# Order edges in the first phase of a three-stage kernel: exponentials behind an eviction, and VectorE side work behind x's low part

## The chip, the cores and the metric

The kernel runs on one core of one Trainium2 chip. The metric is the device time of that core in microseconds (us). A profiled execution has two numbers: its time as a run, and its span, from the first to the last instruction in the trace.

## The reference

Three stages, each feeding the next; batch 4, 576 tokens, width 512.

```python
# 1. attention, 8 heads of 64, a causal window of 128 tokens
scores = 0.125 * q @ k.T + bias          # bias: -slope(head) * |distance|
scores = where(0 <= rel < 128, scores, -1e9)
x = softmax(scores) @ v                  # then [4, 576, 512]
# 2. a gated block
u, v = split(relu(x @ w_in), 2)          # w_in: 512 x 1024
v = (v - mean(v)) / sqrt(var(v) + 1e-6)
v = w_spatial @ v + b_spatial            # mixes the 576 tokens
x = (u * v) @ w_out
# 3. four experts of causal attention (head size 64); each token keeps the two
#    experts of the largest gate logits, weighted by their softmax
```

## The kernel before, in words

**Number form.** Every large product runs on TensorE with fp32 operands split in two: a high part in the rounded type fp32r and a low part, the rest. `split` (L131 to L133) does this for a tile in PSUM: ScalarE (ACT) casts the high part (L132), then VectorE (DVE) subtracts it from the source (`lo_part`, L129).

**The first phase** is the loop of lines 600 to 634. It computes stage 1 and, woven into it, the products of stage 2 up to the spatial mix. A tile is (batch b, tile j): 128 tokens, five tiles to a batch (the last has 64), 20 tiles in all. Step s of the loop does, in program order:

- `attend(tile s-2)`: 32 matmuls of attention weights by v into the PSUM tile px (L415);
- `scores(tile s)`: q by k into two PSUM tiles ps, one for each half g of the heads (L353, L356);
- `take(tile s-2)`: `split` of px into x, the input of stage 2;
- `parts(s)`: one piece of side work; and then, for g = 0 and 1, `transposes(tile s-1, g)` (four TensorE transposes into the PSUM tile pt, L390, evicted by ACT to pT, L391, and cut in two by GpSimd, L398 and L399), `softmax(tile s, g)` (DVE row reductions, L150; ACT exponentials, L151, four to a half; DVE normalisation, L378 to L380), and `parts(s)` again.

`parts` draws on three lists. `late`: chunks 4 to 7 of w_in, of which `bits` (L281 to L289) makes a rounded high part by integer operations on DVE, `add_in` puts it through TensorE with the identity (psw, L218, L219) and a cast (L221), and `low_in` makes the low part (L129). `prep` (steps 6 to 8): the spatial weights wsp, five tiles that come by DMA (L252) into st_wsp, a buffer of two, and are cast on ACT (L254) and subtracted on DVE (L129). `outw` (from step 9): the output weights.

Between these, `dense.pull` draws stage 2: `v_tile` (products pv, L436; relu on ACT, L444; statistics on DVE, L447 and L448; the square root on ACT, L462 and L463, and four small DVE operations, L466 to L469; `scale`, L472; `high`, an ACT cast, L475; `low`, L129), `u_half` (pu, L499; relu L503) and `spatial`.

**Buffers.** pt and px share one PSUM buffer (pool psT, one buffer): the transposes of tile s-1 wait until both halves of `split` have read px, each later use of pt waits for the eviction before it, and px waits for the last of these. The products pv, pu, pg and psw share three (pool psD).

**Order.** TensorE's order is written out by hand. The order on ACT, DVE, GpSimd and the DMA queue is set by a scheduler at build time from its own estimates of durations; an order edge (`tc.issue_after`) makes an instruction stand behind another in the issue order of its engine, without a semaphore.

Of the kernel before, what the change touches and what calls it, by code (L numbers as in the profile page):

```python
# [2 lines left out]

# [6 lines left out]
F32 = mybir.dt.float32  # L10
# [7 lines left out]
ALU = mybir.AluOpType  # L18
# [4 lines left out]
P = 128  # L23
# [79 lines left out]
def block_kernel(ctx, tc, qP, kP, v, w_in, wspT, bsp, w_outT, wcat, wo, rel, relt, low, tri, out):  # L103
    nc = tc.nc
# [21 lines left out]


    def lo_part(lo, src, hi, engine=nc.vector):
        engine.tensor_sub(lo, src, hi.bitcast(F32))  # L129

    def split(hi, lo, src):  # L131
        nc.scalar.copy(hi, src)  # L132
        lo_part(lo, src, hi)  # L133

    def staggered(gens):

# [39 lines left out]
    x = [xg.tile([P, 4, 640], F32R, name=f"x{i}") for i in range(2)]  # L176
    u = [d2.tile([P, S], F32, name=f"u{m}") for m in range(4)]
    vn = [[d2.tile([P, 512], F32R, name=f"vn{i}_{t}") for t in range(5)] for i in range(2)]
# [204 lines left out]
    def transposes(b, j, g):  # L383
        p = st_[b, j, g]
        n = 4 if j < 4 else 2
        pt = psT.tile([P, 4, P], F32, tag="T", name=f"pt{b}_{j}_{g}")
        here = a1.tile([P, 4, P], F32, tag="pT", name=f"pT{b}_{j}_{g}", bufs=4)
        before = None
        for i in range(n):
            nc.tensor.transpose(pt[:, i, :], p[:, i, :], ident)  # L390
        nc.scalar.copy(here[:, :n], pt[:, :n])  # L391
        if j > 0:

            before = a1.tile([P, 4, P], F32, tag="pU", name=f"pU{b}_{j}_{g}", bufs=4)
            w = P if j < 4 else 64
            m = 4
            u_, h = (t[:, :n].rearrange("p i (o q) -> p (i o) q", q=w) for t in (before, here))
            nc.gpsimd.affine_select(out=u_, in_=h, pattern=[[0, m], [-1, w]], compare_op=ALU.is_gt, fill=0.0, base=0, channel_multiplier=1)  # L398
            nc.gpsimd.affine_select(out=h[:w], in_=h[:w], pattern=[[0, m], [1, w]], compare_op=ALU.is_ge, fill=0.0, base=0, channel_multiplier=-1)  # L399
        st_[b, j, g] = (before, here)  # L400
# [18 lines left out]
    def take(b, j, px):  # L419
        q0, qn = TOK[j]  # L420
        if j < 4:
            split(x[0][:, :, q0 : q0 + P], x[1][:, :, q0 : q0 + P], px)
        else:
            twice = [t[:, :, 512:640].rearrange("p m (r c) -> p m r c", r=2) for t in x]
            split(*twice, px[:, :, :64].unsqueeze(2).to_broadcast([P, 4, 2, 64]))
        xready[b, j] = now[0] + (b == 0)

    stats_, vr = {}, {}

    def v_tile(b, t):  # L430
        t0 = TOK[t][0]
        pv = psD.tile([P, 512], F32, tag="D", name=f"pv{b}_{t}")
        n = 0
        for i, j in PASSES:
            for k in range(4):
                nc.tensor.matmul(pv, x[i][:, k, t0 : t0 + P], win[j][:, k, 512:1024], start=(n == 0), stop=(n == 11))  # L436
                n += 1
            if n < 12:
                yield 4 * 216
        if t == 0:  # L440
            stats_[0] = d2.tile([P, 5, 10], F32, tag="vs", name=f"vs{b}", bufs=2)
        st = stats_[0]
        vr[t] = d2.tile([P, 512], F32, tag="vr", name=f"vr{b}_{t}", bufs=3)
        nc.scalar.activation(vr[t], pv, AF.Relu)  # L444

        def stats():
            nc.vector.bn_stats(st[:, t, 0:6], vr[t])  # L447
            nc.vector.bn_aggr(st[:, t, 6:8], st[:, t, 0:6])  # L448

        dense.post.append(stats)  # L450
        if t in (2, 4):
            tiles = range(0, 3) if t == 2 else range(3, 5)
            dense.post.extend(normalised(st, tiles))
        yield 4 * 216

    def normalised(st, tiles):
# [12 lines left out]
            nc.vector.tensor_mul(y, y, z)  # L469

        def scale(t):
            nc.vector.tensor_scalar(vr[t], vr[t], st[:, t, 6:7], st[:, t, 8:9], op0=ALU.subtract, op1=ALU.mult)  # L472

        def high(t):
            nc.scalar.copy(vn[0][t], vr[t])  # L475
# [1 line left out]
        def low(t):  # L477

            r = slice(64, 128) if t == 4 else slice(0, 128)
            lo_part(vn[1][t][r], vr[t][r], vn[0][t][r])  # L480
            if t == 4:
                nc.scalar.copy(vn[1][t][0:64], vr[t][0:64])
                nc.gpsimd.tensor_scalar(vn[0][t][64:97], pad[64:97].to_broadcast([33, 512]), 1.0, 0.0, op0=ALU.mult, op1=ALU.add)
# [43 lines left out]
    tiles = [(b, j) for b in range(B) for j in range(5)]  # L527
    prep = setup()
# [29 lines left out]
    late = late_chunks()  # L558

    def parts(s):  # L560

        next(late, None)
        for _ in range(2 if 6 <= s < 9 else 0):
            next(prep, None)
        if s >= 9:
            next(outw, None)


    warm(22)
# [17 lines left out]
    px = attend(0, 0)  # L587
# [16 lines left out]
    outw = iter(())  # L604
    for s in range(2, len(tiles) + 2):
# [3 lines left out]
        if s == 9:  # L609
            early_stack.close()  # L610
            outw = out_weights(right.enter_context(tc.tile_pool(name="later", bufs=1, side="right")))
        if s > 2:
# [3 lines left out]
            px = attend(b, j)  # L616
# [9 lines left out]
        for g in range(2):  # L626
            if 1 <= s <= len(tiles):
                transposes(*tiles[s - 1], g)
            dense.pull(RATE / 6)
            if s < len(tiles):  # L630
                softmax(*tiles[s], g)
            now[0] += 1
            dense.pull(RATE / 6)
            parts(s)
# [321 lines left out]
    px = None  # L956
# [104 lines left out]
```

## Time and profile before

| | |
|---|---|
| time, median of 3 runs | 515.16 us (515.05 to 515.49) |
| time of the profiled execution | 514.89 us |
| its span | 513.2 us |
| mean granted TensorE clock | 0.988 |
| TensorE matmul busy | 488.0 us (95%) |
| VectorE busy | 308.4 us (60%) |
| ScalarE busy | 261.8 us (51%) |
| GpSimd busy | 98.4 us (19%) |

The profiled execution took 514.89 us as a run, 1.69 us more than its span. Busy times overlap. The granted clock is the share of TensorE's full clock that the chip allowed, averaged over the span.

### The profile page before, as it was taken

The page shows a single profiled execution, that of the slowest core. Times are in us where ns is not written, and L with a number is a line of the kernel's source. Part 1 is how long each engine was busy: PE and PEld are TensorE (multiplying, and loading weights), DVE is VectorE, ACT ScalarE, POOL GpSimd, SP SyncE. Part 2 cuts the span into 40 slices and gives each one's busy share as a digit, 9 for nine tenths or more (in the row PEclk, how much of TensorE's full clock was granted, in tenths as well). Part 3 has the DMA queues.
Part 4 walks back from the last instruction along what each step waited for, and adds up shares of the span by engine and source line. Part 5 has one row for each costly group of instructions (what it writes and reads, how often), then busy time and mean ns, then how long its engine had stood idle before and what let it go on. Part 6 is the DMA issues. An engine that isn't in the chain of part 4 may idle for free. (4 is left out here: it accounts for less than half of the span.)

```text
span 513.2 us, 10541 instructions
## 1 busy us (share of the span) xinstructions
PE 488.0 (95%) x3910; PEld 425.5 (83%) x3910; DVE 308.4 (60%) x1069; ACT 261.8 (51%) x778; POOL 98.4 (19%) x205
## 2 busy tenths in 40 slices
PE   8879889999999999999999999989989999999995
PEld 6547668898988989899888999978978898897784
DVE  4978877555878768785455525264574564562441
ACT  4764567533656337463344314264564554546652
POOL 0012210222102211012211010122322333232121
PEclk9997989999999999999999999999999999999999
DMA  8931223325231451301206640230000000003321
GB/s 283 372 128 42 63 87 102 114 70 181 91 94 43 180 189 42 94 2 52 104 1 193 198 158 5 90 93 1 1 1 3 2 1 1 1 2 116 112 103 42
DMA packets 25079, 44.34 MB, mean 86 GB/s; under 512 B 5826, under 2 KB 8258, under 8 KB 24644
## 3 DMA queue, kind: packets, MB, share of 16 engines
q1 hardware_dynamic: 24868, 43.54, 25.4%
q8 instruction: 31, 0.51, 0.4%
q10 hardware_dynamic: 160, 0.13, 0.1%
q14 instruction: 20, 0.16, 0.1%
HBM read 32.13 MB, written 11.53 MB: 85 GB/s over the span
## 5 line engine op out<-in xcount | busy, mean ns | idle before, releaser
L151 ACT ACTIVATE p<-p,st 128x128 f32<-128x128 f32 x144 | 56.3, 392 | 38.0 <-DVE st L150 38.0
L436 PE MATMUL pv<-win,x 128*128 128x512 f32 x240 | 63.9, 409 | 0.7 <-ACT x L132 0.7
L780 PE MATMUL pq<-x,W 128*128 128x288 f32 x384 | 59.4, 303 | 0.9 <-DVE k L129 0.8
L516 PE MATMUL pg<-wsp,vn 128*128 128x288 f32 x384 | 58.9, 298 | 0.1
L780 PEld LDWEIGHTS pq<-x,W 128*128 128x128 f32 x384 | 52.1, 188 | 4.8 <-issue 2.3
L499 PE MATMUL pu<-x,win 128*128 128x288 f32 x384 | 55.1, 298 | 0.0
L398 POOL TENSOR_SCALAR_AFFINE_SELECT pU<-pT 128x512 f32<-128x512 f32 (+1 forms) x32 | 22.6, 706 | 168.1 <-ACT pT L391 164.1
L158 POOL TENSOR_SCALAR pB<-pB,stB 128x128 f32<-128x128 f32 (+4 forms) x72 | 39.0, 560 | 80.1 <-DVE stB L868 65.5
L516 PEld LDWEIGHTS pg<-wsp,vn 128*128 128x128 f32 x384 | 52.9, 188 | 1.3 <-issue 1.0
L499 PEld LDWEIGHTS pu<-x,win 128*128 128x128 f32 x384 | 52.0, 188 | 1.8 <-issue 0.5
L436 PEld LDWEIGHTS pv<-win,x 128*128 128x128 f32 x240 | 43.9, 192 | 9.8 <-issue 1.0
L151 ACT ACTIVATE pB<-pB,stB 128x128 f32<-128x128 f32 (+3 forms) x64 | 35.6, 558 | 13.6 <-DVE stB L150 13.6
L150 DVE CUSTOM_DVE_ANT_0 pB<-psB,trit 128x128 f32<-128x128 f32 (+3 forms) x64 | 28.3, 485 | 11.1 <-PE psB L845 10.5
L888 PE MATMUL ptB<-ident,pB 128*128 128x128 f32 (+1 forms) x200 | 31.1, 274 | 3.9 <-POOL pB L158 3.6
L804 PE MATMUL pvB<-W,x 128*128 128x260 f32 (+1 forms) x240 | 34.7, 289 | 0.0
L804 PEld LDWEIGHTS pvB<-W,x 128*128 128x128 f32 (+1 forms) x240 | 30.1, 178 | 1.1 <-issue 1.1
L927 PE MATMUL pout<-wo,o 128*128 128x512 f32 x108 | 30.1, 410 | 1.0 <-ACT o L132 1.0
L353 PE MATMUL ps<-k,q 64*128 64x256 f32 (+1 forms) x256 | 29.8, 374 | 0.8 <-DMA k<-in_kP 0.8
L390 PE MATMUL pt<-ident,p 128*128 128x128 f32 x144 | 22.9, 277 | 7.8 <-DVE x L129 6.1
L888 PEld LDWEIGHTS ptB<-ident,pB 128*128 128x128 f32 (+1 forms) x200 | 23.7, 139 | 7.6 <-POOL pB L158 4.7
L150 DVE CUSTOM_DVE_ANT_0 p<-ps,relm 128x128 f32<-128x128 f32 x128 | 29.5, 286 | 0.7 <-DMA relm<-in_rel 0.2
L415 PE MATMUL px<-pT,v 128*64 128x128 f32 (+1 forms) x320 | 29.6, 276 | 0.0
(147 smaller groups left out, 882.0 us busy)
## 6 DMA issues: line engine op xcount, KB each, us to landing
q<-in_qP SPq DMA_DIRECT2D x20, 256.0 KB, 3.0
g_dram<-g SPq DMA_DIRECT2D x16, 288.0 KB, 2.1
raw<-in_w_in SPq DMA_DIRECT2D x8, 512.0 KB, 6.8
v<-in_v SPq DMA_DIRECT2D x16, 256.0 KB, 3.2
gf<-g_dram SPq DMA_DIRECT2D x4, 1024.0 KB, 5.3
out<-ot SPq DMA_DIRECT2D x16, 256.0 KB, 2.0
k<-in_kP SPq DMA_DIRECT2D x3, 1152.0 KB, 5.3
rawo<-in_w_outT SPq DMA_DIRECT2D x4, 512.0 KB, 4.3
```

Source lines behind the costliest of these rows:

```text
L150: nc.vector.tensor_tensor_reduce(s_view, ps_view, tab, -0.125, FLT_MAX, ALU.add, ALU.min, nm)
L151: nc.scalar.activation(s_view, s_view, AF.Exp, bias=nm, scale=-1.0, accum_out=sm)
L158: nc.gpsimd.tensor_scalar(p, p, r, 0.0, op0=ALU.mult, op1=ALU.add)
L353: nc.tensor.matmul(ps[:, o, 256 * h : 256 * h + kn], Q_[b, j][r, hp, :], K_[b][r, hp, k0 : k0 + kn], start=True, stop=True)
L415: nc.tensor.matmul(px[64 * o : 64 * o + 64, hp, :qn], V_[b, t][:kb, h * 64 : h * 64 + 64], rhs, start=(t == max(0, j - 1)), stop=(t == j))
L436: nc.tensor.matmul(pv, x[i][:, k, t0 : t0 + P], win[j][:, k, 512:1024], start=(n == 0), stop=(n == 11))
L499: nc.tensor.matmul(pu[:, :HALF], win[i][:, k, m * P : (m + 1) * P], x[j][:, k, c], start=(n == 0), stop=(n == 11))
L516: nc.tensor.matmul(pg[:, :HALF], vn[i][k][:, m * P : (m + 1) * P], wsp[j][:, k, c], start=(n == 0), stop=False)
L780: nc.tensor.matmul(pq[:, :HALF], W[i][:, k, c0 : c0 + P], G[j][:, k, c], start=(n == 0), stop=(n == 11))
L804: nc.tensor.matmul(pv[:tn, :260], G[i][:, k, COL[t] : COL[t] + tn], W[j][:, k, 512:772], start=(n == 0), stop=(n == 11))
L888: nc.tensor.transpose(pt[:kb, n, :], p[pr][:, o, c0 : c0 + kb], ident)
L927: nc.tensor.matmul(po[:tn], o2[i][:, pr, :tn], wos[j][:, pr, :], start=(n == 0), stop=(n == 5))
```

## The change

It adds order edges in the first phase and no operation. `transposes` keeps the instruction of its eviction (L391) in `turned[g]`, and the loop traces `softmax` of the next tile's half g under an order edge on it, so that its ACT instructions (the exponentials) stand behind the eviction in ACT's order. `take` keeps the low part of x (on DVE) in `taken`, and statistics, scale and low part of v, and everything in `parts`, are traced under an order edge on that: their DVE instructions stand behind x's low part, which was traced before them.

```diff
     def lo_part(lo, src, hi, engine=nc.vector):
-        engine.tensor_sub(lo, src, hi.bitcast(F32))
+        return engine.tensor_sub(lo, src, hi.bitcast(F32))
     def split(hi, lo, src):
         nc.scalar.copy(hi, src)
-        lo_part(lo, src, hi)
+        return lo_part(lo, src, hi)
+    taken, turned = [None], {}
+    def behind(ins):
+        return tc.issue_after(ins.ins) if ins is not None else nullcontext()
...
-        nc.scalar.copy(here[:, :n], pt[:, :n])
+        turned[g] = nc.scalar.copy(here[:, :n], pt[:, :n])
...
-            split(x[0][:, :, q0 : q0 + P], x[1][:, :, q0 : q0 + P], px)
+            taken[0] = split(x[0][:, :, q0 : q0 + P], x[1][:, :, q0 : q0 + P], px)
...
-            split(*twice, px[:, :, :64].unsqueeze(2).to_broadcast([P, 4, 2, 64]))
+            taken[0] = split(*twice, px[:, :, :64].unsqueeze(2).to_broadcast([P, 4, 2, 64]))
...
         def stats():
-            nc.vector.bn_stats(st[:, t, 0:6], vr[t])
-            nc.vector.bn_aggr(st[:, t, 6:8], st[:, t, 0:6])
+            with behind(taken[0]):
+                nc.vector.bn_stats(st[:, t, 0:6], vr[t])
+                nc.vector.bn_aggr(st[:, t, 6:8], st[:, t, 0:6])
...
         def scale(t):
-            nc.vector.tensor_scalar(vr[t], vr[t], st[:, t, 6:7], st[:, t, 8:9], op0=ALU.subtract, op1=ALU.mult)
+            with behind(taken[0]):
+                nc.vector.tensor_scalar(vr[t], vr[t], st[:, t, 6:7], st[:, t, 8:9], op0=ALU.subtract, op1=ALU.mult)
...
-            lo_part(vn[1][t][r], vr[t][r], vn[0][t][r])
+            with behind(taken[0]):
+                lo_part(vn[1][t][r], vr[t][r], vn[0][t][r])
...
     def parts(s):
-        next(late, None)
-        for _ in range(2 if 6 <= s < 9 else 0):
-            next(prep, None)
-        if s >= 9:
-            next(outw, None)
+        with behind(taken[0]):
+            next(late, None)
+            for _ in range(2 if 6 <= s < 9 else 0):
+                next(prep, None)
+            if s >= 9:
+                next(outw, None)
...
             if s < len(tiles):
-                softmax(*tiles[s], g)
+                with behind(turned.get(g)):
+                    softmax(*tiles[s], g)
```

The scheduler then orders all engines but TensorE anew. TensorE's and GpSimd's orders come out unchanged; 130 rows of ACT's order and 240 of DVE's differ. Lines of the changed kernel stand six or more further down (L391 becomes L397, L151 L157, L444 L450, L254 L260, L284 to L289 become L290 to L295). Numbers in the names are batch, tile and half: p0_2_1 is batch 0, tile 2, half 1.

**Place A**, ACT, step 4 of the loop, where tile (0,1) is transposed (pt0_1_0, pt0_1_1) and the exponentials of tile (0,2) are taken. Before:

```order
L391 COPY pT0_1_0_409<-pt0_1_0_408 128x512
L444 ACTIVATE vr0_0_423<-pv0_0_392 128x512
L151 ACTIVATE p0_2_1_455,st0_2_1_456<-p0_2_1_455,st0_2_1_456 128x128 x3
L221 CAST win0_100<-psw4_441 128x512
L151 ACTIVATE p0_2_1_455,st0_2_1_456<-p0_2_1_455,st0_2_1_456 128x128
L391 COPY pT0_1_1_446<-pt0_1_1_445 128x512
L281 ACTIVATE f6_551<-raw6_361 128x512
```

With the change:

```order
L397 COPY pT0_1_0_409<-pt0_1_0_408 128x512
L157 ACTIVATE p0_2_0_427,st0_2_0_428<-p0_2_0_427,st0_2_0_428 128x128 x4
L450 ACTIVATE vr0_0_423<-pv0_0_392 128x512
L227 CAST win0_100<-psw4_441 128x512
L397 COPY pT0_1_1_446<-pt0_1_1_445 128x512
L157 ACTIVATE p0_2_1_455,st0_2_1_456<-p0_2_1_455,st0_2_1_456 128x128 x4
L287 ACTIVATE f6_551<-raw6_361 128x512
```

Both evictions have moved ahead of the exponentials of their half; the cast of w_in's chunk 4 (L221) still stands between relu and the second eviction.

**Place B**, DVE, step 6 of the loop, which takes x of tile (0,2) (px0_2) and whose `parts` round chunk 7 of w_in (f7, u3, raw7, win1). Before:

```order
L284 TENSOR_SCALAR f7_625<-f7_625 128x512
L285 TENSOR_SCALAR u3_109<-f7_625 128x512
L286 SCALAR_TENSOR_TENSOR u3_109<-raw7_368,u3_109 128x512
L288 TENSOR_SCALAR f7_625<-u3_109 128x512
L129 TENSOR_TENSOR x1_105<-px0_2_595,x0_104 128x4x128
L365 COPY_PREDICATED ps0_4_0_612<-lowt_99,ps0_4_0_612 128x2x64
L289 SCALAR_TENSOR_TENSOR win1_101<-raw7_368,f7_625 128x512
```

With the change, where between the last two rows but five stand the eight rows of the reductions L156 of p0_4_0 and p0_4_1 (left out):

```order
L129 TENSOR_TENSOR x1_105<-px0_2_595,x0_104 128x4x128
L129 TENSOR_TENSOR win1_101<-psw6_590,win0_100 128x512
L290 TENSOR_SCALAR f7_625<-f7_625 128x512
L371 COPY_PREDICATED ps0_4_0_612<-lowt_99,ps0_4_0_612 128x2x64
L371 COPY_PREDICATED ps0_4_1_615<-lowt_99,ps0_4_1_615 128x2x64
L291 TENSOR_SCALAR u3_109<-f7_625 128x512
...
L292 SCALAR_TENSOR_TENSOR u3_109<-raw7_368,u3_109 128x512
L384 TENSOR_SCALAR st0_4_0_643<-st0_4_0_643 128x2
L294 TENSOR_SCALAR f7_625<-u3_109 128x512
L385 RECIPROCAL st0_4_0_643<-st0_4_0_643 128x2
L295 SCALAR_TENSOR_TENSOR win1_101<-raw7_368,f7_625 128x512
```

The low part of x is now first; the whole rounding of chunk 7, and the low part of chunk 6 (win1<-psw6), have moved behind it, the last of the rounding behind the reductions too.

**Place C**, ACT, step 8, where x of tile (0,4) is taken (px0_4), `prep` casts the spatial weights (wsp0<-st_wsp) and tile (1,0) is transposed (pt1_0_0, pt1_0_1). Before:

```order
L444 ACTIVATE vr0_3_782<-pv0_3_759 128x512
L132 CAST x0_104<-px0_4_803 128x4x128
L254 CAST wsp0_102<-st_wsp0_836 128x576
L254 CAST wsp0_102<-st_wsp1_839 128x576
L151 ACTIVATE p1_1_0_848,st1_1_0_849<-p1_1_0_848,st1_1_0_849 128x128 x3
L391 COPY pT1_0_0_842<-pt1_0_0_841 128x512
L151 ACTIVATE p1_1_0_848,st1_1_0_849<-p1_1_0_848,st1_1_0_849 128x128
L254 CAST wsp0_102<-st_wsp2_873 128x576
L151 ACTIVATE p1_1_1_901,st1_1_1_902<-p1_1_1_901,st1_1_1_902 128x128 x3
L391 COPY pT1_0_1_880<-pt1_0_1_879 128x512
```

With the change:

```order
L450 ACTIVATE vr0_3_782<-pv0_3_759 128x512
L260 CAST wsp0_102<-st_wsp0_836 128x576
L132 CAST x0_104<-px0_4_803 128x4x128
L260 CAST wsp0_102<-st_wsp1_839 128x576
L260 CAST wsp0_102<-st_wsp2_873 128x576
L260 CAST wsp0_102<-st_wsp3_877 128x576
L397 COPY pT1_0_0_842<-pt1_0_0_841 128x512
L157 ACTIVATE p1_1_0_848,st1_1_0_849<-p1_1_0_848,st1_1_0_849 128x128 x4
L260 CAST wsp0_102<-st_wsp4_937 128x576
L397 COPY pT1_0_1_880<-pt1_0_1_879 128x512
L157 ACTIVATE p1_1_1_901,st1_1_1_902<-p1_1_1_901,st1_1_1_902 128x128 x4
L450 ACTIVATE vr0_4_890<-pv0_4_862 128x512
```

The eviction of pt1_0_0 now stands ahead of its exponentials, and behind two more casts of the spatial weights, those of st_wsp2 and st_wsp3. The relu of tile (0,4) (vr0_4) stands behind the fifth cast and the second half's exponentials.

## Rows read from the trace of the kernel before

**Rows 1.** Page: busy us of each engine, share of the span, instructions.

```profile
PE 488.0 (95%) x3910; PEld 425.5 (83%) x3910; DVE 308.4 (60%) x1069; ACT 261.8 (51%) x778; POOL 98.4 (19%) x205
```

**Rows 2.** Waits of TensorE, 28 to 100 us: us in total, times, longest.

```profile
PE pt L390 <- DVE x L129: 5.0, 3, 3.7
PE px L415 <- ACT pT L391: 2.6, 1, 2.6
PE psw L219 <- DVE win L289: 0.8, 1, 0.8
```

**Rows 3.** The same view, 100 to 300 us.

```profile
PE pt L390 <- DVE x L129: 1.2, 2, 0.9
...
PE pt L390 <- ACT pT L391: 0.6, 1, 0.6
```

**Rows 4.** Windows: length, busy us PE, PEld, DVE, ACT, POOL, PEclk, DMA share, GB/s.

```profile
22.50:25.00 2.50, 1.72 (x5) 0.81 (x6) 1.85 (x6) 2.43 (x10) 0.00 (x0) 1.00 1.02 398
37.50:40.00 2.50, 2.10 (x20) 2.13 (x22) 2.43 (x7) 0.83 (x2) 1.27 (x2) 0.50 0.00 0
40.00:42.50 2.50, 2.50 (x20) 2.03 (x18) 2.36 (x6) 0.58 (x1) 0.00 (x0) 0.50 0.11 34
42.50:45.00 2.50, 2.50 (x15) 1.78 (x12) 1.84 (x7) 0.24 (x1) 0.00 (x0) 0.71 0.22 78
67.50:70.00 2.50, 2.50 (x9) 1.92 (x9) 1.76 (x11) 2.50 (x14) 0.82 (x2) 0.57 0.00 0
70.00:72.50 2.50, 2.50 (x21) 1.63 (x19) 1.40 (x4) 1.14 (x4) 1.15 (x2) 0.75 0.00 0
```

**Rows 5.** Timeline, 34 to 38 us: start, us, instruction, idle before and releaser.

```profile
34.75 0.60 PE L390 MATMUL pt<-ident,p 128*128 128x128 f32 x4
...
36.33 0.56 ACT L221 CAST win<-psw 128x512 fp32r<-128x512 f32 x1
...
37.19 0.56 ACT L391 COPY pT<-pt 128x512 f32<-128x512 f32 x1
...
37.90 0.70 PE L415 MATMUL px<-pU,v 128*64 128x128 f32 x4 [2.55 <-ACT pT L391]
```

**Rows 6.** Timeline, 52 to 58 us.

```profile
53.99 0.68 DVE L129 TENSOR_TENSOR x<-px,x 128x512 fp32r<-128x512 f32 x1
...
54.78 0.68 DVE L289 SCALAR_TENSOR_TENSOR win<-raw,f 128x512 fp32r<-128x512 uint32 x1
...
57.53 0.80 PE L219 MATMUL psw<-win,one 128*128 128x512 f32 x1
```

**Rows 7.** Windows, the stretch of place B.

```profile
51.40:57.70 6.30, 5.86 (x47) 4.63 (x43) 5.78 (x20) 3.30 (x11) 1.73 (x3) 1.00 0.28 83
```

**Rows 8.** Timeline, 62 to 67 us.

```profile
63.25 1.66 ACT L475 CAST vn<-vr 128x512 fp32r<-128x512 f32 x3 [1.42 <-DVE vr L472]
...
64.82 0.58 ACT L132 CAST x<-px 128x512 fp32r<-128x512 f32 x1
...
66.59 0.44 PE L390 MATMUL pt<-ident,p 128*128 128x128 f32 x2 [3.72 <-DVE x L129]
```

**Rows 9.** Timeline, 74 to 83 us, the stretch of place C.

```profile
74.38 0.69 DVE L129 TENSOR_TENSOR x<-px,x 128x512 fp32r<-128x512 f32 x1 [1.14 <-ACT x L132]
...
76.36 5.31 SPq L252 DMA_DIRECT2D st_wsp<-in_wspT  x4
...
78.37 0.66 PE L390 MATMUL pt<-ident,p 128*128 128x128 f32 x4 [0.30 <-ACT pT L391]
...
82.22 0.59 ACT L444 ACTIVATE vr<-pv 128x512 f32<-128x512 f32 x1
```

**Rows 10.** Tile st_wsp: the casts that read it (ns, starts), and its DMAs.

```profile
L254 ACT CAST wsp<-st_wsp x5: 659/673/674, 74.2 to 84.0; 128x576 fp32r<-128x576 f32 x5
...
DMA to landing us min/median/max: 2.6/2.8/3.7
```

**Rows 11.** Page, groups: the first phase's exponentials (busy us, mean ns; idle before, releaser).

```profile
L151 ACT ACTIVATE p<-p,st 128x128 f32<-128x128 f32 x144 | 56.3, 392 | 38.0 <-DVE st L150 38.0
```

More of the change, by code (lines that the diff above doesn't have):

```diff
@@ L1 @@
 from collections import deque
-from contextlib import ExitStack
+from contextlib import ExitStack, nullcontext
 import concourse.bass as bass
```

## Prediction

> **What bounds the kernel now.** I read the busy times first, then TensorE's waits, then the timeline and the windows around each wait. TensorE is busy for 95% of the span, the next engine for 60% [rows 1]: the kernel is bound by TensorE, and only what lets TensorE stand still or run slowly can be won. No operation is added or removed, so matmul time at full clock stays. What the change can touch lies in the first phase, up to about 300 us. There the list of waits is short. From 28 to 100 us TensorE waits 5.0 us, in three pieces, for the low part of x (the transposes use the PSUM buffer that x is read from), of which one piece is 3.7; 2.6 us once for an eviction of transposes on ACT; and 0.8 once for a rounded chunk of w_in [rows 2]. From 100 to 300 us it waits 1.2 us in two pieces for x's low part and 0.6 once for an eviction [rows 3]. The waits of the two kinds that the change speaks to, x's low part and evictions, come to 9.4 us: that is what there is to take.
>
> The second thing to see is the granted clock. After the pause of 2.6 us the clock stands at 0.50 in two windows of 2.5 us and at 0.71 in the third; after the one of 3.7 us at 0.57 and 0.75 [rows 4]. TensorE is busy there all the while, on the same matmuls, so half a clock costs half the window: 1.25 + 1.25 + 0.73, less 0.2 for the 0.4 us in which it was idle anyway, is 3.0 us for the first fall; 1.08 + 0.63 = 1.7 us for the second. Each long pause thus costs about its own length again.
>
> **The change, place A** (the 2.6 us pause). ACT cast psw at 36.33 and evicted the second transposes at 37.19, though TensorE had written them by 35.35 (34.75 + 0.60), and px, which needs the same buffer, began at 37.90, 0.71 after the eviction's start [rows 5]. Between stood exponentials of 0.39 us [rows 11], now all behind the eviction. What is left ahead of it is the cast of psw, whose matmuls stand right ahead of the transposes of 34.75 on TensorE: I let it start at 35.0, 0.56 long, so the eviction starts at 35.6 and px at 35.6 + 0.71 = 36.3. **-1.55 us**, between -2.55 (the cast no hindrance) and 0.
>
> *The clock after A.* With 0.80 + 0.95 us idle instead of 0.80 + 2.55 I take the clock to stay up: the window at 22.5 us, with 1.72 of 2.50 busy, that is 0.78 idle, kept it at 1.00 [rows 4]. **-3.0 us**, the other end 0.
>
> **Place B** (chunk 7 of w_in). DVE used to round the chunk while it waited for x's cast: four pieces before x's low part at 53.99, and the last, 0.68 at 54.78, right behind; TensorE took the chunk at 57.53, 3.5 us after x's low part began [rows 6]. Now x's low part comes first and all of the rounding stands behind it, with the low part of chunk 6 and the reductions of tile (0,4) between. DVE has 5.78 us of work in the 6.30 us of this stretch [rows 7], of which about 2 us filled the wait for x; that hole now stays empty, so the chunk comes 5.1 us after x's low part instead of 3.5. **+1.4 us** for TensorE (its 0.2 of slack taken off); bounds 0 (TensorE has that much other work that I missed) and 2.3 (the whole hole, and a piece more).
>
> **The 3.7 us pause.** ACT cast three parts of normalised v in 1.66 us, from 63.25, ahead of x's cast at 64.82; transposes began at 66.59 [rows 8]. Now one of the three casts is ahead: 2 x 0.55 = 1.1 less. Against it, two exponentials (0.39 each [rows 11]) now stand ahead of the relu from which the statistics of v come: +0.8. On DVE x's low part no longer stands behind the low parts of v: it started at 66.59 - 0.68 = 65.9 while the cast was done at 65.4, so -0.5. **-0.8 us**, between -1.6 and +0.5. A pause of 2.9 us is left, and with it, I take it, the fall of the clock (1.7).
>
> **Place C** (spatial weights). The casts of st_wsp2 and st_wsp3 now stand ahead of the eviction of pt1_0_0, and their data are not there yet: the buffer has two slots, so the third DMA can go only when DVE has made the low part of the first tile. That DMA was issued at 76.36, 2.0 after x's low part at 74.38 [rows 9]; the new order puts the low part of st_wsp0 right behind x's (which took 0.69, as I take this one to), so it is issued at 74.38 + 2 x 0.69 = 75.8, and the next at 76.5. Landing takes 2.6 to 3.7 us, 2.8 in the middle [rows 10]: st_wsp3 is there at 79.3, its cast (0.67) done at 80.0, the eviction at 80.5, and pt1_0_1, which began at 78.37 after a wait of 0.30, follows then. **+2.2 us**; the lower end 0.3, if the data come by the time the eviction is due; the upper 3.1, with the landing of 3.7.
>
> The fifth cast and four exponentials now also stand ahead of the relu of tile (0,4), which ran at 82.22 [rows 9]; that relu frees one of three PSUM buffers that the products of u_half wait for. 0.67 + 4 x 0.39 = 2.2 us later. TensorE has products in the other two buffers meanwhile, so I take 0.7 of it: **+1.55 us**, between 0 (all covered) and 2.2.
>
> **The small ones.** Of the 1.3 us in the other two waits for x's low part before 100 us [rows 2] one stays (place B) and one goes, **-0.6**. The 1.2 and 0.6 us after 100 us [rows 3] end at instructions that now come first, **-1.8**; bounds 0 and -1.8. GpSimd's order is the same and it has 81% to spare; the order on the DMA queue changes by one swap behind the phase, at no cost.
>
> **Sum:** -1.55 - 3.0 + 1.4 - 0.8 + 2.2 + 1.55 - 0.6 - 1.8 = -2.6 us. The profiled execution took 514.89, so 512.3; the median of the three runs, 515.16, stands 0.27 above it: **512.6 us**. A measurement of this kernel can tell about 0.2%, 1.0 us, from no change.
>
> **The rivals.**
>
> *R1, place C costs nothing.* The spatial weights land before the casts are reached, or the pulled products cover the wait: both terms at their lower ends, 0.3 and 0 in place of 2.2 and 1.55, so 512.6 - 3.45 = 509.1. For it: six DMAs only, and the queue's share in the stretches read is small. Against: before, ACT waited for this very data though it asked later [rows 9, 10].
>
> *R2, the change doesn't do what it says at A.* The pause shrinks, and the clock falls all the same: 512.6 + 3.0 = 515.6, no change. For it: two pauses, 0.80 and about 0.95, stand close together there. Against: 0.78 idle of 2.50 did no harm [rows 4]. The Trainium skill ("TensorE: Matmul & The Clock Gate", "A second HAM failure mode: psum-queue depth-cycling") says that short idle spells between groups of matmuls, when they are frequent, make the clock swing between its levels without one long gap. By that rule this rival holds, and the time is 515.6; the window at 22.5 us, one such spell, does not agree with it, but holds one spell and not two.
>
> *R3, the other side: the clock falls at place C.* The new pause, 2.5 us with the old 0.30, is as long as the one at A that lowered the clock. If it lowers it too, the same 3.0 us of half clock come back, and with the landing at 3.7 in place of 2.8 another 0.9: 512.6 + 3.0 + 0.9 = 516.5, slower. It decides from the point where C costs 3.6 us more than in my sum (1.0 above 515.16). For it: both pauses above 2.5 us in this trace were followed by a fall [rows 2, 4]. Against: at A 0.8 us of idle time stood right before, which C lacks, and four transposes and eight products run just ahead of it at full clock.
>
> **How the numbers follow.** Forecast 0.45, with a range of its own from 511.2 (the 3.7 us pause, now 2.9, no longer drops the clock, -1.7, some of it given back) to 514.0 (B and the relu at their upper ends); R1 0.15; R2 0.2; R3 0.2. The range, 509.5 to 517.0, leaves out about half of R1 and the upper part of R3, 0.17 together. Faster: nearly all of the forecast and R1, 0.58. Same: most of R2 and pieces of the others, 0.20. Slower: most of R3 and the rest of R2, 0.22.
>
> **What the profile after would show.** Right: no wait of px for an eviction above 1.2 us near 36 us; PEclk 1.00 in the ten us after it; the px groups there shorter than the 0.70 us of before [rows 5]; a wait of psw for win of over 1 us near 55; a wait of TensorE for an eviction of about 2.5 us near 75, and ACT idle before a cast of st_wsp for a DMA; no waits above 0.3 us for x between 100 and 300 us. Wrong: PEclk below 1 near 37 (R2), or below 1 in the 5 us after the pause at C (R3); no wait at C (R1). A new long wait at a line that I have not named would overturn the sum.

## The result: slower, and where the time went

| | before | changed |
|---|---|---|
| first comparison, median | 515.25 us (515.05 to 515.49, 4 runs) | 523.41 us (519.63 to 524.13, 4 runs) |
| ratio, 95% interval | | 1.0143 [1.0095, 1.0192] |
| repeated beside e9 and e10, median | 515.71 us (515.00 to 518.35, 17 runs) | 519.72 us (518.39 to 521.58, 7 runs) |
| ratio, 95% interval | | 1.0060 [1.0036, 1.0083] |
| profiled execution of the first comparison | 514.89 us | 524.13 us |
| its mean granted clock | 0.988 | 0.979 |

The forecast was 512.6 us with a range to 517.0. The change is slower in both comparisons, by 8.2 and by 4.0 us. At one granted clock the two agree: the one run of the first comparison with a mean of 0.989 took 519.63 us and the one of the second with 0.989 took 519.72, where 31 of 34 runs of the kernel before with 0.989 took 514.8 to 515.8. The other three of the first comparison had 0.979 and took 523.39 to 524.13. So about 4 us go with the order, and the 3.7 us between the two medians go with the clock. In the loop's own variable s, places A, B and C are at s = 2, 4 and 6; the step numbers in the section on the change are two too high.

The page of the changed kernel:

```profile
span 522.4 us, 10547 instructions
...
PE 492.2 (94%) x3910; PEld 428.6 (82%) x3910; DVE 310.1 (59%) x1069; ACT 259.5 (50%) x778; POOL 99.3 (19%) x205
```

The matmuls are the same 3910 in the same order; TensorE is busy 4.2 us longer, which is slower clock, and the rest of the 9.2 us by which the span grew (513.2 to 522.4) is idle time. Its waits, first from 28 to 100 us (to be held against [rows 2]), then from 100 to 300 us (against [rows 3]):

```profile
PE pt L396 <- DVE x L129: 3.7, 2, 3.4
PE pt L396 <- ACT pT L397: 2.5, 1, 2.5
PE psw L225 <- DVE win L295: 1.3, 1, 1.3
PE psw L224 <- DVE u L292: 0.9, 1, 0.9
PE px L421 <- ACT pT L397: 0.8, 1, 0.8
PE px L421 <- POOL pT L405: 0.6, 1, 0.6
```

```profile
PE pg L525 <- ACT vn L483: 2.2, 1, 2.2
PE pt L396 <- ACT pT L397: 1.0, 1, 1.0
PE pg L530 <- POOL vn L492: 0.9, 1, 0.9
PE pt L396 <- DVE x L129: 0.7, 2, 0.5
```

Early, the waits changed places and did not get less (8.7 us before, which is [rows 2] and the 0.30 of [rows 9]; 9.8 now). Later two waits, 3.1 us together, appear at the spatial mix of batch 3, which had none.

Since TensorE's order is the same, one matmul can be followed from one timeline to the other. The starts of six groups in the changed kernel, and two waits between them (34.87 and 54.45):

```profile
34.87 0.51 PE L225 MATMUL psw<-win,one 128*128 128x512 f32 x1 [1.26 <-DVE win L295]
...
36.63 0.44 PE L421 MATMUL px<-pU,v 128*64 128x128 f32 x4 [0.82 <-ACT pT L397]
...
47.28 0.44 PE L421 MATMUL px<-pU,v 128*64 128x128 f32 x4
...
54.45 1.13 PE L224 MATMUL psw<-u,ident 128*128 128x512 f32 x2 [0.91 <-DVE u L292]
...
55.64 0.50 PE L225 MATMUL psw<-win,one 128*128 128x512 f32 x1
...
64.04 0.69 PE L396 MATMUL pt<-ident,p 128*128 128x128 f32 x2 [3.36 <-DVE x L129]
...
79.21 0.66 PE L396 MATMUL pt<-ident,p 128*128 128x128 f32 x4 [2.49 <-ACT pT L397]
...
300.27 1.76 PE L525 MATMUL pg<-wsp,vn 128*128 128x288 f32 x12
```

Before, the six started at 37.90 [rows 5], 50.67, 57.53 [rows 6], 66.59 [rows 8], 78.37 [rows 9] and 292.38 us:

```profile
50.67 0.44 PE L415 MATMUL px<-pU,v 128*64 128x128 f32 x4
...
292.38 1.76 PE L516 MATMUL pg<-wsp,vn 128*128 128x288 f32 x12
```

So the changed kernel is 1.3 us ahead at A, 3.4 ahead at 47 us, 1.9 at 55, 2.6 at 64, then 0.8 **behind** at 79 and 7.9 behind at 300. The remaining 1.3 us come after that, most of them where the clock is at half near 353 us. The granted clock of the changed kernel, in the stretches in which it was at half (columns as in [rows 4]):

```profile
63.30:70.10 6.80, 6.06 (x16) 4.44 (x16) 6.25 (x25) 4.39 (x19) 2.33 (x4) 0.50 0.21 77
80.40:83.80 3.40, 3.40 (x15) 3.28 (x14) 1.69 (x11) 2.25 (x9) 0.00 (x0) 0.50 0.56 177
288.60:295.40 6.80, 5.91 (x25) 5.59 (x25) 4.79 (x8) 3.65 (x7) 0.62 (x1) 0.50 0.05 13
353.40:356.80 3.40, 3.37 (x14) 2.87 (x14) 0.44 (x2) 0.65 (x2) 2.66 (x7) 0.50 0.03 5
```

After A the clock stayed up; it fell towards the end of the pause for x, after place C, between the two new waits of the spatial mix, and right after a wait of 1.93 us for GpSimd that ended at 353.24. The same wait, 1.92 us to 345.33, stood in the kernel before, and no fall followed it there.

**The end of the phase, which the prediction did not look at.** ACT's order around the last casts of v, before:

```
L503 ACTIVATE u1_107<-pu3_1_1_3197 128x288
L475 CAST vn0_3_113<-vr3_3_3134 128x512
L475 CAST vn0_4_114<-vr3_4_3171 128x512
L482 CAST vn1_4_119<-vr3_4_3171 64x512
L503 ACTIVATE u2_108<-pu3_2_1_3214 128x288
L132 CAST wc02_3281<-st_wc2_3303 128x772
```

With the change:

```
L512 ACTIVATE u1_107<-pu3_1_1_3197 128x288
L132 CAST wc02_3281<-st_wc2_3303 128x772
L483 CAST vn0_3_113<-vr3_3_3134 128x512
L483 CAST vn0_4_114<-vr3_4_3171 128x512
L491 CAST vn1_4_119<-vr3_4_3171 64x512
```

The cast of a weight chunk of stage 3 (wc) has moved ahead of the casts of v, though the change puts no edge on it. Timelines, before and changed:

```profile
280.74 1.14 ACT L475 CAST vn<-vr 128x512 fp32r<-128x512 f32 x2 [0.24 <-DVE vr L472]
...
283.09 1.74 PE L516 MATMUL pg<-wsp,vn 128*128 128x288 f32 x12
283.57 0.84 ACT L132 CAST wc<-st_wc 128x772 fp32r<-128x772 f32 x1 [0.86 <-DMA st_wc<-in_wcat]
...
284.67 0.43 PE L521 MATMUL pg<-wsp,vn 97*128 97x288 f32 x2
```

```profile
281.81 1.00 DVE L480 TENSOR_SCALAR vr<-vr,vs 128x512 f32<-128x512 f32 x2
284.74 0.56 PE L525 MATMUL pg<-wsp,vn 128*128 128x288 f32 x3
286.12 0.83 ACT L132 CAST wc<-st_wc 128x772 fp32r<-128x772 f32 x1 [3.96 <-DMA st_wc<-in_wcat]
...
286.86 1.14 ACT L483 CAST vn<-vr 128x512 fp32r<-128x512 f32 x2
...
287.52 1.69 PE L525 MATMUL pg<-wsp,vn 128*128 128x288 f32 x9 [2.22 <-ACT vn L483]
...
290.10 0.85 PE L530 MATMUL pg<-wsp,vn 97*128 97x288 f32 x2 [0.89 <-POOL vn L492]
```

ACT stands 3.96 us before a cast whose DMA has not landed, with the casts of v, whose input VectorE's scaling (from 281.81, 1.00 us) had ready, queued behind it. From the first pg to the L530 group it takes 290.10 - 284.74 = 5.4 us where it took 284.67 - 283.09 = 1.6: 3.8 us, of which 3.1 are the two waits and the rest is the clock that falls at 288.60. A second profile of the changed kernel (e11 below) shows the swap without a fall of the clock:

```profile
285.41 0.56 PE L525 MATMUL pg<-wsp,vn 128*128 128x288 f32 x3
...
297.59 1.76 PE L525 MATMUL pg<-wsp,vn 128*128 128x288 f32 x12
```

Its first pg comes 2.3 us later than before (283.09), and the group that began at 292.38 comes 5.2 later: the swap by itself costs 2.9 us.

### The profile page after: what moved, and what is told of

Read it like the earlier page. It is cut to its first block, busy times and chain, and to the rows that moved or that the text cites. A ratio compares the mean times of both kernels' runs of the same rounds, so it can differ in the third digit from the quotient of the medians.

```text
span 522.4 us, 10547 instructions
## 1 busy us (share of the span) xinstructions
PE 492.2 (94%) x3910; PEld 428.6 (82%) x3910; DVE 310.1 (59%) x1069; ACT 259.5 (50%) x778; POOL 99.3 (19%) x205
## 5 line engine op out<-in xcount | busy, mean ns | idle before, releaser
L442 PE MATMUL pv<-win,x 128*128 128x512 f32 x240 | 65.2, 416 | 0.7 <-ACT x L132 0.7
L525 PE MATMUL pg<-wsp,vn 128*128 128x288 f32 x384 | 61.2, 305 | 2.2 <-ACT vn L483 2.2
L791 PE MATMUL pq<-x,W 128*128 128x288 f32 x384 | 60.5, 307 | 0.9 <-DVE k L129 0.8
L157 ACT ACTIVATE p<-p,st 128x128 f32<-128x128 f32 x144 | 56.2, 395 | 8.3 <-DVE st L156 8.3
L525 PEld LDWEIGHTS pg<-wsp,vn 128*128 128x128 f32 x384 | 55.2, 195 | 3.5 <-ACT vn L483 2.5
L791 PEld LDWEIGHTS pq<-x,W 128*128 128x128 f32 x384 | 53.2, 192 | 4.8 <-issue 2.3
L508 PE MATMUL pu<-x,win 128*128 128x288 f32 x384 | 56.4, 302 | 0.0
L508 PEld LDWEIGHTS pu<-x,win 128*128 128x128 f32 x384 | 53.5, 193 | 1.9 <-issue 1.2
L397 ACT COPY pT<-pt 128x512 f32<-128x512 f32 (+1 forms) x40 | 21.6, 541 | 42.0 <-PE pt L396 42.0
L157 ACT ACTIVATE pB<-pB,stB 128x128 f32<-128x128 f32 (+3 forms) x64 | 35.6, 558 | 13.8 <-DVE stB L156 13.8
L156 DVE CUSTOM_DVE_ANT_0 pB<-psB,trit 128x128 f32<-128x128 f32 (+3 forms) x64 | 28.3, 485 | 11.1 <-PE psB L856 10.5
L129 DVE TENSOR_TENSOR x<-px,x 128x512 fp32r<-128x512 f32 x20 | 13.8, 690 | 30.9 <-ACT x L132 30.7
L156 DVE CUSTOM_DVE_ANT_0 p<-ps,relm 128x128 f32<-128x128 f32 x128 | 29.6, 285 | 1.4 <-DMA relm<-in_rel 0.2
```

What stands on the lines that cost most here:

```text
L156: nc.vector.tensor_tensor_reduce(s_view, ps_view, tab, -0.125, FLT_MAX, ALU.add, ALU.min, nm)
L157: nc.scalar.activation(s_view, s_view, AF.Exp, bias=nm, scale=-1.0, accum_out=sm)
L508: nc.tensor.matmul(pu[:, :HALF], win[i][:, k, m * P : (m + 1) * P], x[j][:, k, c], start=(n == 0), stop=(n == 11))
L525: nc.tensor.matmul(pg[:, :HALF], vn[i][k][:, m * P : (m + 1) * P], wsp[j][:, k, c], start=(n == 0), stop=False)
L791: nc.tensor.matmul(pq[:, :HALF], W[i][:, k, c0 : c0 + P], G[j][:, k, c], start=(n == 0), stop=(n == 11))
```

## Experiments

All runs of e1 to e4, of e5 to e8, of e9 to e11 and of e12 to e14 shared the runs of the kernel before, which had medians of 515.69, 515.65, 515.71 and 515.51 us. "Changed" is the changed kernel. Ratios are to the kernel before.

**e1: the weights of stage 3 behind v** (changed, plus one edge).

```diff
+                cast[0] = nc.scalar.copy(vn[1][t][0:64], vr[t][0:64])
...
     while later:
         dense.pull(1000.0)
-        later.popleft()()
+        with behind(cast[0]):
+            later.popleft()()
```

> The changed kernel with one more order edge: the ACT casts of the combined weights of stage 3 (wc, chunks 2 and 3) stand behind the last cast of v of batch 3, as they did before the change. Theory T1 (the largest single loss is the end of the first phase, where the cast of the third chunk, which waits for its DMA, stands ahead of the casts of v of batch 3): the waits of pg there (2.2 and 0.9 us) go, and the fall of the clock after them; 523.4 falls by 5 to 6.5 us, to about 517.5, with the clock of that stretch at 1.00. Rival T2 (the loss is the clock's own and comes back at another place): the waits go but the time stays above 521. Rival T3 (the wait there is hidden by other work): 523.

Measured: 517.41 us (12 runs), ratio 1.0028 [1.0009, 1.0046]. That is 6.0 below the first median of the changed kernel and 2.3 below the repeated one; at the same mean clock, 0.989, its two runs took 516.94 and 517.01, 2.7 below the changed kernel's 519.63 and 519.72. In its timeline the casts of v run first, pg goes through without a wait, and the cast of wc waits behind them:

```profile
281.48 1.14 ACT L483 CAST vn<-vr 128x512 fp32r<-128x512 f32 x2 [0.23 <-DVE vr L480]
...
283.83 1.74 PE L525 MATMUL pg<-wsp,vn 128*128 128x288 f32 x12
...
284.97 0.84 ACT L132 CAST wc<-st_wc 128x772 fp32r<-128x772 f32 x1 [1.52 <-DMA st_wc<-in_wcat]
...
293.11 1.76 PE L525 MATMUL pg<-wsp,vn 128*128 128x288 f32 x12
```

It stands 0.7 us behind the kernel before at its first pg (283.83 against 283.09) and still 0.7 at the later group (293.11 against 292.38): here the mix costs nothing.

T1 holds: the largest single loss is that swap, and it comes back nowhere else. By the comparison at one clock it is worth 2.7 us; what the first median of the changed kernel adds to this is its lower clock. 1.7 us of loss against before stay.

**e2 to e4: place C and place B mended.** e2 is changed, plus casts of the spatial weights behind the latest eviction; e3 adds e1's edge; e4 takes `late` out of the edge on x's low part as well.

```diff
-    def parts(s):
+    def parts(s, g=None):
         with behind(taken[0]):
             next(late, None)
-            for _ in range(2 if 6 <= s < 9 else 0):
-                next(prep, None)
+            with behind(turned.get(g)):
+                for _ in range(2 if 6 <= s < 9 else 0):
+                    next(prep, None)
...
-            parts(s)
+            parts(s, g)
```

> The changed kernel with one more order edge: the ACT casts of the spatial weights stand behind the eviction of the last transposes traced before them. T1: the wait of 2.5 us of pt1_0_1 near 77 us goes, and the fall of the clock at 80.4 us with it, together 3.5 to 4 us: 519.5. T2: under 1 us, as a later wait of the spatial mix for these weights takes its place.

> Both edges of e1 and e2 on the changed kernel. T1 (the two losses are separate and add up): 523.4 - 6 - 3.8 = 513.6, slightly faster than before (515.2). T2: above 517.

> As e3, and the pieces of w_in (chunks 4 to 7) no longer stand behind x's low part. T1: the waits of 0.9 and 1.3 us for chunk 7 near 55 us go down to what they were, 1.2 to 1.5 us in all: 512.2. Rival: the pause for x's low part gets that much longer again and nothing is won against e3.

Measured: e2 520.77 us (6 runs), ratio 1.0094 [1.0068, 1.0121]; e3 518.27 (12 runs), 1.0051 [1.0037, 1.0066]; e4 520.73 (6 runs), 1.0098 [1.0071, 1.0124]. The wait at pt1_0_1 went, and nothing was won: e3 is no faster than e1. e2's timeline shows where the wait went:

```profile
86.43 1.14 ACT L483 CAST vn<-vr 128x512 fp32r<-128x512 f32 x2 [1.41 <-DVE vr L480]
...
88.12 0.67 ACT L273 CAST wsp<-st_bias 32x576 fp32r<-32x576 f32 x1
88.81 0.67 ACT L274 CAST bias_hi<-st_bias 1x576 fp32r<-1x576 f32 x1
...
90.11 0.59 ACT L132 CAST x<-px 128x512 fp32r<-128x512 f32 x1
...
91.48 0.66 PE L396 MATMUL pt<-ident,p 128*128 128x128 f32 x4 [2.90 <-DVE x L129]
```

TensorE is done with the work ahead of the next transposes 4.8 us earlier than in the changed kernel (at 88.58 against 93.40), but x's cast, which stands behind v's casts and the two of the spatial bias (st_bias) on ACT, only 2.1 earlier (90.11 against 92.17): 2.90 us of wait one step on. T1's sum for C failed; "a later wait takes its place" was right, only at x and not at the mix; e3's T2 (above 517) held with it. In e4 the chunk's rounding stands ahead of x's low part again, and the wait for x, 0.24 us in e3, is 2.94 near 54 us: no gain from B by itself, and its rival held. (Of the two waits that its expectation puts near 55 us only the one of 0.9 is there; the one of 1.3 is at 34.87, place A.)

**e11: the changed kernel again.**

> The changed kernel, unedited, beside the same runs of the kernel before as e9 and e10, to have its spread: T1 takes its times to differ by where the clock falls, in steps of about 1.5 us, between 519.5 and 524, with the span shorter the higher the granted clock; rival: one value within 0.3%.

Measured: 519.72 us (518.39 to 521.58, 7 runs): T1 held in kind, over a range that begins 1 us lower. The runs go with the clock: the three at a mean clock of 0.992 took 518.39 to 518.84 us, the one at 0.982 took 521.58. In its profile the clock fell after A, which it had not in the first, and not after the spatial mix, which it had. The order of a kernel does not settle where the clock falls; what its order settles is the waits, and these were nearly the same: 1.24 in place of 2.22 us at pg, where TensorE arrived 0.7 us later and the DMA landed 0.3 earlier, and no second wait behind A, where the clock was at half.

**e5 and e6: place A alone.** The kernel before with the edge on the exponentials at s = 2 (e5), at s = 2 and 3 (e6); no edge on x's low part.

```diff
-                softmax(*tiles[s], g)
+                with behind(turned.get(g) if s in (2, 3) else None):
+                    softmax(*tiles[s], g)
```

> The kernel before with a single order edge of the change: the exponentials of tile (0,2) behind the eviction of tile (0,1), at s = 2 of the loop, nothing else. The scheduler moves six rows of ACT's order for it: those at place A, and, 250 us further on, the cast of the third chunk of stage 3's weights to a place ahead of the casts of v of batch 3. T1 (that swap alone costs the waits at the end of the phase and the clock behind them): minus 1.3 to 1.6 at A (minus up to 3 more where the clock used to fall), plus 3.8, plus 1.7 to 3.4: 517 to 521. T2 (the loss at the end of the phase needs the rest of the change): 514.

> As e5, with the edge at s = 3 too (exponentials of tile (0,3) behind the eviction of tile (0,2)). Here the scheduler keeps the order at the end of the phase as it was before. T1: place A alone: 515.7 - 1.3 to 1.6 = 514.3, and down to 511.5 where the clock no longer falls near 37 us. Rival (what A gains is lost at the next wait for x's low part): 515.7.

Measured: e5 519.45 us (6 runs), ratio 1.0067 [1.0051, 1.0083]; e6 517.49 (10 runs), 1.0035 [1.0022, 1.0049]. e5 shows two things. The swap at the end of the phase (2.1 us of waits at pg in its profile) needs one edge 250 us earlier and no more; with the second edge of e6 the scheduler's order there is again that of before. And A's gain does not last: the transposes that began at 54.73 before begin at 54.81. T1's total (517 to 521) thus came out, but not from its terms: A gives nothing in the end, the swap costs 2.6 us (0.7 behind at 283.09, 3.3 at 292.38), and no fall of the clock follows it. For e6 the rival held in kind, at a time 1.8 above its 515.7: in its profile 0.7 us stand at 274 us and 1.5 come with a fall of the clock near 347 that the profile of before has not. In e6, where the later orders are those of before, px starts at 36.65 as in the changed kernel, and then:

```profile
50.15 0.59 ACT L132 CAST x<-px 128x512 fp32r<-128x512 f32 x1 [0.26 <-PE px L421]
...
52.92 0.69 DVE L295 SCALAR_TENSOR_TENSOR win<-raw,f 128x512 fp32r<-128x512 uint32 x1
53.53 0.68 DVE L129 TENSOR_TENSOR x<-px,x 128x512 fp32r<-128x512 f32 x1
...
54.27 1.12 PE L396 MATMUL pt<-ident,p 128*128 128x128 f32 x4 [2.67 <-DVE x L129]
```

x's cast is done at 50.74, but VectorE, with no gap from 48.4 us on, works through the end of a normalisation, v's statistics, chunk 6's low part and the rounding of chunk 7 first. What TensorE won at A it waits here.

**e12: the same with chunk 7 not rounded** (e6; four of the five VectorE operations left out).

```diff
+        if n == 7:
+            nc.scalar.activation(f, live[n][0].bitcast(I32)[:, 1::2].bitcast(F32), AF.Abs)
+            nc.vector.scalar_tensor_tensor(in_parts(n)[1], live[n][0].bitcast(I32)[:, 0::2].bitcast(U32),
+                                           2.0**-52, f, op0=ALU.mult, op1=ALU.mult)
+            return
```

> The kernel of e6 (place A's gain, order at C and at the end of the phase as before), with four of the five VectorE operations that round chunk 7 of w_in left out (1.97 us of VectorE in e6's timeline; the chunk's values are not those of the reference then). T1 (what A gains is lost at the transposes of tile (0,3) because VectorE, without a pause there, has to work off the rounding before x's low part): the wait there, 2.67 in e6, falls by about 2, and the time by 1.5 to 2.5, to about 515.5. Rival (that wait is set by the cast of x on ACT, or by px): within 0.5 of e6's 517.5.

Measured: 513.98 us (12 runs), ratio 0.9974 [0.9959, 0.9988], 3.5 below e6.

```profile
51.44 0.68 DVE L129 TENSOR_TENSOR x<-px,x 128x512 fp32r<-128x512 f32 x1
...
52.18 0.66 PE L400 MATMUL pt<-ident,p 128*128 128x128 f32 x4 [0.82 <-DVE x L129]
```

The wait falls by 1.85 us, from 2.67 to 0.82, for 1.97 us of VectorE: T1 held, and it is VectorE's queue that holds this stretch. The rest of the 3.5 was not forecast and goes at least in part with the clock: e6's profile has four stretches of 3.4 us at half clock (near 37, 54, 67 and 347 us), e12's two (near 63 and 272).

**e8 and e10: each half of the change alone.** e8: exponentials behind evictions, nothing behind x's low part. e10: the reverse.

```diff
-            with behind(taken[0]):
...
-        with behind(taken[0]):
-            next(late, None)
+        next(late, None)
```

```diff
-                with behind(turned.get(g)):
-                    softmax(*tiles[s], g)
+                softmax(*tiles[s], g)
```

> Half of the change: exponentials behind evictions at every step, nothing behind x's low part. Spatial weights' casts (place C) and the cast of stage 3's weights stand as badly as in the changed kernel. T1: B goes (1.4 less), the rest stays: 522. Rival (the edges on x's low part are what costs): below 517.

> The other half of the change: statistics, scale and low part of v and the side work behind x's low part; exponentials free. Stage 3's weights stand ahead of the casts of v of batch 3, as in the changed kernel. T1 (this half costs the wait for chunk 7, 1.4, and through the scheduler the end of the phase, 3.8 and its clock; it wins 0.8 before 70 us and 1.2 after 100): 515.7 + 1.4 + 1.5 (place C) + 3.8 + 2 - 2 = 522. Rival (the halves cost only together): 516.

Measured: e8 527.27 us (4 runs), ratio 1.0224 [1.0209, 1.0238]; e10 521.16 (6 runs), 1.0090 [1.0066, 1.0114]. e8 is 5 us slower than T1 said, so neither T1 nor its rival held, and slower than the whole change: without the edges on x's low part, TensorE waits 12.7 us in 28 to 310 us for x's low part, in seven pieces (4.6 in e1, which has both halves). e10's T1 (522) held within 1 us. The halves are not additive: the edges on x's low part are what keeps part of A's gain, and by themselves they win nothing.

**e7: edges up to s = 4, v behind x, `parts` free, e1's edge.**

```diff
-                with behind(turned.get(g)):
+                with behind(turned.get(g) if s < 5 else None):
...
-        with behind(taken[0]):
-            next(late, None)
+        next(late, None)
...
+        with behind(cast[0]):
+            later.popleft()()
```

> Exponentials behind evictions up to s = 4; statistics, scale and low part of v behind x's low part throughout; the side work of `parts` free; the casts of stage 3's weights behind those of v of batch 3. Spatial weights and w_in's chunk 7 stand as before the change. T1 (places A and the later waits gain, B, C and the end of the phase cost nothing): 515.7 - 1.5 at A - 1.5 later, less what the clock gives: 510 to 513. Rival: 515 to 516, the gain at A going into the pause near 63 us.

Measured: 518.80 us (5 runs), ratio 1.0061 [1.0047, 1.0076]. T1 was wrong by 6 us, and the rival by 3: orders that are each as before at C and at the end still give the gain at A back at the transposes of tile (0,3) (2.94 us of wait for 0.44) and more near 70 us, where two evictions of transposes cost 1.74 and 0.53.

**e9: the change from s = 7 on only, with e1's edge.**

```diff
+        if now[0] >= 28:
+            taken[0] = low
...
-                with behind(turned.get(g)):
+                with behind(turned.get(g) if s >= 7 else None):
...
+        with behind(cast[0]):
+            later.popleft()()
```

> The change kept only from s = 7 of the loop on (edges of exponentials and of x's low part alike), and the casts of stage 3's weights behind those of v of batch 3. The orders of the first 75 us are those of before. T1 (the early steps are held by VectorE and ScalarE, so edges there only move the wait; the late waits of 0.8, 0.6, 0.3 and 0.9 us are single ones with idle engines round them and can be won): 515.7 - 0.7 - 1.8 = 513.2, faster than before. Rival (here too each wait comes back at the next step): 515 to 516.

Measured: 514.60 us (512.88 to 518.72, 12 runs), ratio 0.9986 [0.9960, 1.0012]. Of the waits of [rows 3], 1.8 us, 0.7 are left, and the profiled span is 511.5 us. The median is 1.1 below that of before, between T1 (513.2) and the rival (515 to 516), and the spread does not tell it from no change. At like clocks the few runs there are point to a gain: 513.84 at 0.988, where the kernel before has 515.56 and 515.75. It is the best version here that leaves nothing out.

**e13 and e14: a maximum on GpSimd.** e9, with the first rounding operation of chunks 4 to 7 on GpSimd; e14 adds the edges at s = 2 and 3.

```diff
-        nc.vector.tensor_scalar(f, f, F32_LEAST, None, op0=ALU.max)
+        (nc.gpsimd if late_ else nc.vector).tensor_scalar(f, f, F32_LEAST, None, op0=ALU.max)
```

> The kernel of e9 with the first operation of the rounding (a maximum) of chunks 4 to 7 on GpSimd, which is idle there: four times 0.42 us less on VectorE between 28 and 57 us. T1 (VectorE holds this stretch): 0.4 to 1.5 us less than e9's 514.6. Rival (the hand-over to GpSimd and back puts the chunk later than it was): 0 to 1.5 us more.

> As e13, with the edges of exponentials at s = 2 and 3 too (place A). T1: with 0.42 us less a chunk, some of A's 1.3 us is kept: 0.3 to 1 us below e13. Rival: as in e6, A's gain is lost at the next wait for x's low part and the time is e13's or up to 2 us more.

Measured: e13 516.44 us (12 runs), ratio 1.0020 [1.0004, 1.0037]; e14 519.62 (6 runs), 1.0075 [1.0053, 1.0097]. The rivals held, and both losses, 1.8 us against e9 and 3.2 against e13, are above their bounds of 1.5 and 2. The maximum takes 1.48 us on GpSimd against 0.42 on VectorE, and TensorE's wait for a rounded chunk near 36 us is 2.29 where it was 0.80 [rows 2].

## Why the prediction was wrong, point by point

Numbers are those of the first profile of the changed kernel.

- **Place A.** Forecast -1.55, measured -1.27 (36.63 against 37.90). Right in kind; the rounded chunk of that place came later too, so psw waited 1.26 in place of 0.80.
- **The clock after A.** Forecast -3.0; from 1.3 to 3.4 us ahead is -2.1. In e11's profile the clock fell there all the same, for about half as long as before: R2 is neither right nor wrong for this order: of the eleven profiles here with these waits at A (psw 1.24 to 1.26, px 0.82), three show a fall there (e3, e6, e11) and eight none.
- **Place B.** Forecast +1.4; from 3.4 to 1.9 ahead is +1.5, as a wait of 0.91 of psw, at the chunk's first part (u, L292) and not, as forecast, at its last (win). Right in size.
- **The 3.7 us pause.** Forecast -0.8; the pause went from 3.72 to 3.36, -0.4, and the start of the group from 1.9 to 2.6 ahead. Right in sign. But the clock was then at half for 6.8 us where the forecast kept the old fall: one more us lost.
- **Place C.** Forecast +2.2; the wait went from 0.30 to 2.49. Right, by the mechanism given: casts of spatial weights waiting for their DMA, ahead of the eviction, as ACT's timeline of the changed kernel shows:

```profile
77.14 0.67 ACT L260 CAST wsp<-st_wsp 128x576 fp32r<-128x576 f32 x1 [3.56 <-DMA st_wsp<-in_wspT]
...
78.58 0.58 ACT L397 COPY pT<-pt 128x512 f32<-128x512 f32 x1
```

R3's second half, the fall of the clock after it, came too, in both profiles.

- **The relu of tile (0,4).** Forecast +1.55, measured 0. The relu did come 2.2 us later, as worked out (84.46 against 82.22), but pu did not wait for it: the lower end of the bounds was right, and the share taken for it was a guess.
- **The small ones.** The -0.6 near 92 us came. The -1.8 after 100 us did not: [rows 3] hold 1.8 us, the changed kernel 1.7 at the same two kinds of wait. The forecast looked at the exponentials, which are now behind these evictions, and not at what stands ahead of them still. In the longest, 1.04 us, it is the cast of an output weight (ho), and this waits for VectorE's rounding of that weight, which the change has put behind x's low part. In e9's order the eviction comes ahead of that cast, and the wait is gone; 1.1 of the 1.8 us are won there. The changed kernel, then e9:

```profile
163.67 0.62 ACT L319 CAST ho<-wo 128x512 fp32r<-128x512 f32 x1 [3.67 <-DVE wo L314]
...
164.50 0.58 ACT L397 COPY pT<-pt 128x512 f32<-128x512 f32 x1
```

```profile
159.25 0.59 ACT L397 COPY pT<-pt 128x512 f32<-128x512 f32 x1 [0.76 <-PE pt L396]
...
162.90 0.62 ACT L319 CAST ho<-wo 128x512 fp32r<-128x512 f32 x1 [0.18 <-DVE wo L314]
```

- **The step that failed** is the end of "the small ones": from 100 us on the sum went by the waits that the old profile listed and took every other difference of ACT's order as free. It named only GpSimd's and the DMA queue's orders there. The swap of the wc cast ahead of v's was in ACT's order to be seen, its row of before even showed ACT waiting for that DMA (0.86 us), and it cost 2.9 us without a fall of the clock (e11) and 6.2 with one, in the first profile: from 1.65 us behind (284.74 against 283.09) to 7.9. e1 shows it: with that one order put back, the time is 2.7 us lower at the same clock, and 2.3 to 6.0 by the medians.
- **The rival on the slower side** was put at C, 0.9 us and the clock. Its sign was right, its place only in part.

Summed at 283 us, the forecast of -2.6 was off by 4.2 us: 0.3 at A, 0.9 at its clock, about 1.0 and 1.5 (estimates, half of the added time at half clock) at the clock after the pause and after C, 1.7 of late waits not won, 0.4 of small differences, less the 1.55 of the relu. Even a perfect reading of the places named would thus have given about +1.7, no gain.

What stays open: why the clock fell at 353 us in the first profile, in stage 3, behind a wait of 1.9 us for GpSimd that the kernel before has too (the profiles of e2, e4, e6, e7 and e14 show such a fall near 350 as well, those of e1, e9 and e11 do not); and why three of the first four runs of the changed kernel had a mean clock of 0.979, when none of the seven later ones went below 0.982.

## What to carry to other kernels

Where a scheduler sets the orders, an edge moves instructions far from where it was put: compare the whole order of every engine, and for each swap ask what the instruction now ahead waits for, a DMA above all (the casts of wc and of st_wsp), but also another engine (the cast of ho); the waits of the old profile say nothing of it. Where runs differ by the granted clock, compare them at the same clock too: it parts what the order costs from what the clock adds. A wait of the bound engine is worth removing only if the next one it meets moves as well: near 50 us VectorE had no gap, and TensorE's gain was paid back at the next transposes until some of VectorE's own work was taken away (e12).

## What was not expected of the hardware

One kernel's runs differ by where the clock falls: e9's twelve runs go from 512.88 us at a mean granted clock of 0.992 to 518.72 at 0.979, and those of the kernel before from 515.0 at 0.989 to 518.35 at 0.982. Two profiles of the changed kernel, with the same waits early on, show the clock at half in different places. The pause at place C shows it best: 2.49 us in the changed kernel was followed by a fall within 1.2 us, 2.60 in e8 (to 81.06) by none before 165 us. So a pause near the length that was followed by a fall (2.55 us [rows 5], 2.49 here) is a chance of 1.5 to 3 us, not a fixed price; the 1.5 and 3 are estimates, half of the 3.4 and 6.8 us that such falls lasted, less the idle time in them.
